# Talking-heads attention and two MLPs on one core: one bank for two head pairs' values, four banks for the first head mixing, and new numbers in the planner

## The chip, the cores and the metric

The kernel runs on one core of a Trainium2 chip. The metric is the device time of one execution in microseconds (us); lower is better. The engines are named as the profile names them: PE (TensorE matmul), PEld (its weight loads), DVE (VectorE), ACT (ScalarE), POOL (GpSimd), SP (SyncE, which issues the DMAs here). PSUM, the memory that PE writes, has eight banks of 512 float32 per partition, and every bank of this kernel belongs to a named ring.

## The reference

```python
B, H, S, D = 4, 12, 448, 64                     # q, k, v: [B, H, S, D]; w_pre, w_post: [H, H]
scores = np.matmul(q, k.transpose(0, 1, 3, 2)) / np.sqrt(D)
scores = np.einsum('bhij,hg->bgij', scores, w_pre)        # first mixing of the heads
scores = scores - np.max(scores, axis=-1, keepdims=True)
attn = np.exp(scores)
attn = attn / (np.sum(attn, axis=-1, keepdims=True) + 1e-09)
attn = np.einsum('bhij,hg->bgij', attn, w_post)           # second mixing of the heads
x = np.matmul(attn, v)                                    # the values
x = x.transpose(0, 2, 1, 3).reshape(B * S, H * D)         # [1792, 768]
h = x @ w_in;  x = (h * np.cos(h)) @ w_out                # first MLP, 2048 wide
return np.maximum(np.maximum(x @ w1, x @ w2), x @ w3) @ w_out2
```

## The kernel before

A batch's 448 rows are cut into four **scores**, blocks of 10 to 12 times 10 rows. For a score, `qk` multiplies queries and keys, two heads at a time (six per score, into two banks of the ring `ps_x`), `evac` copies each head from its bank to SBUF (on ACT or DVE), and `send` writes it by DMA into the grid `t`, where row and head lie side by side on the partitions.

A score is then worked off in **visits**, two slots of 10 rows at a time (92 in all, four of them with one slot). In a visit `mix1` (L575) mixes the heads into two banks of `ps_m`, `rowmax` (DVE) and `soft` (ACT, the exponential with its sum) make two tiles `e`, `guard`, `recip` and `wscale` (DVE) divide the second mixing's weights by the sums (tile `w2s`), `mix2` (L616) mixes again into one bank of `ps_t` for each slot, both of which it needs from its start, and `keep` (ACT or DVE) copies each bank into the buffer `a2`.

When a **stretch** of visits is complete (two scores, 220 or 230 rows), `av` (L640) multiplies its `a2` with the values, one pair of heads after the other in steps of two pairs; `keepx` (ACT or DVE, two copies a pair, tile `xs`) puts rows back in order, and `out` writes them to `xT` in memory.

Every instruction's place is set by a planner (`Plan.run`) when the kernel is built: it plays the operations through with the occupancy of each engine given in `add` (in us, `"T"` for PE, `"A"` ACT, `"V"` DVE, `"D"` DMA), a delay until the result is seen (`lands`, or one delay per engine), the rings of banks and buffers (`takes`, `frees`), a rank, and orders that must hold (`after`, `behind`). Each engine then executes its instructions in the written order and waits at whatever is not ready. An instruction waits for what the compiler found it to depend on, which need not be what the planner thought.

At the end of attention, when the last `send` has been issued, the buffers of scores are given up to the first MLP (`open_early`): its weights are fetched and cut in two parts on ACT, DVE and POOL, `xget` reads back the tokens of the first batch (in a place of `t` that the last score but one leaves free), and its matmuls (L156 to L158) fill PE between the last visits. From some point on PE runs matmuls of the MLPs without a gap.

Of the kernel before, what the change touches and what calls it, by code (L numbers as in the profile page):

```python
# [21 lines left out]
RI = 10  # L22
# [3 lines left out]
HALVES = [[[10, 12], [12, 11]]] * B  # L26
NHALF = 230
RT = 12
RH = RI // 2
BUFS = {"k": 10, "q": 9, "s": 8, "e": 5, "w2s": 3, "v": 7, "xs": 6, "a2": 2, "ps_m": 3, "ps_t": 3, "ps_x": 2}  # L30
# [413 lines left out]
def attention(ctx, tc, q, k, v, w_pre, w_post, same_row, xT, tp, mlps):  # L444
# [36 lines left out]
    for b, sizes in enumerate(HALVES):  # L481
        i = 0
        for n, half in enumerate(sizes):
            start, column = i, 0
            for slots in half:
                i = min(i, S - RI * slots)
                score.append((b, i, RI * slots, slots, 2 * b + n, column))
# [143 lines left out]
    def av(half, x, _):  # L631
        b, _, _, m, _ = halves[half]
        a2 = live["a2", half]
        for hp in pairs(x):
            vt = live["v", b, hp]
            live["av", hp] = ps_t.tile([128, JB, H, RI], F32, name="aps")
            ps = live["av", hp] = live["av", hp].rearrange("p j g i -> p (j g i)")
            for j in range(JB):
                for g in range(2):
                    nc.tensor.matmul(ps[64 * g:64 * g + 64, :m], vt[:, j, g, :], a2[:, j, 2 * hp + g, :m],  # L640
# [18 lines left out]
    def add(f, a, rank, engines, after=(), turn=False, **kw):  # L659

        key = f.__name__, *a
        plan.add(key, rank, partial(f, *a), engines, after, behind=before.get(f, ()) if turn else (), **kw)
# [3 lines left out]
    HP = H // 2  # L666

# [7 lines left out]
    for n in range(NS):  # L675
        b = score[n][0]
        start, end = score[n - 1][0] != b or not n, n == NS - 1 or score[n + 1][0] != b
        for hp in range(HP):
# [6 lines left out]
            add(qk, (n, hp), r, {"T": 0.8}, [("qget", b, hp), ("kget", b, hp)], turn=True, takes=[ring] * 2,  # L685
                frees=[(f, (f + "get", b, hp)) for f in "kq"] if end else [])
            for h in range(2 * hp, 2 * hp + 2):
                add(evac, (n, h), r, {"A": 0.55, "V": 0.62}, [("qk", n, hp)], turn=True, takes=[place := copy_place(n, h)[0]], frees=[(ring, ("qk", n, hp), h % 2)])
                if h == 0:
                    plan.add(("new_t", n), r, lambda _: None, {}, [("evac", n, 0)], takes=["t"])  # L690
                add(send, (n, h), r, {"D": score[n][2] / 118.0}, [("evac", n, h), ("new_t", n)], turn=True, frees=[(place, ("evac", n, h))], lands=2.5)


    for y, (n, t, slots) in enumerate(visits):
        i = 2 * y
        key = lambda f, *x: (f, y, *x)
        add(mix1, (y,), i, {"T": 0.8}, [("wmix", 0), ("fill", n % 2)] + [("send", n, h) for h in range(H)], turn=True, takes=["ps_m"] * 2,
            frees=[("t", ("new_t", n))])
# [3 lines left out]
        add(guard, (y,), i, {"V": 0.12}, [key("soft", a) for a in range(2)])  # L702
        add(recip, (y,), i, {"V": 0.12}, [key("guard")])
        add(wscale, (y,), i, {"V": 0.25}, [key("recip"), ("wmix", 1)], turn=True, takes=["w2s"])
        add(mix2, (y,), i + 1.5, {"T": 0.05 + 0.45 * len(slots)}, [key("wscale")], turn=True, takes=["ps_t"] * len(slots),
            frees=[("e", key("soft", a)) for a in range(2)] + [("w2s", key("wscale"))])
# [6 lines left out]
    for half, (b, _, _, _, members) in enumerate(halves):  # L713
        last = (first + [N])[members[-1] + 1] - 1
        ends = [("keep", y, a) for y, x in enumerate(visits) if x[0] in members for a in x[2]]
        start = ends[0]
        for x in range(HP // 2):
            r = last + 2.5 + 3.0 * x
            for hp in pairs(x) if half % 2 == 0 else ():
# [495 lines left out]
```

## Time and profile before

| | us |
|---|---|
| median of 3 runs | 1171.14 (1169.19 to 1177.53) |
| the profiled execution | 1172.04 |
| its span, first to last instruction | 1170.3 |
| PE busy in the span | 1130.7 |
| DVE busy | 992.9 |
| ACT busy | 656.3 |
| attention, until PE runs only MLP matmuls | 387.9 |

A busy PE is not a PE at its best: matmuls are pipelined and their ends are modelled, so a short stall is hidden in a row that looks busy. The time from the start of one group of matmuls to the start of the next says more. The granted clock of PE was 0.996 of full speed over the span.

### The profile page before, as it was taken

The numbers are of one execution on the slowest core, as the hardware profiler recorded it, in microseconds if no ns is written. First come the engines' busy times: TensorE is split into PE (matmuls) and PEld (weight loads), VectorE is DVE, ScalarE is ACT, GpSimd is POOL, SyncE is SP. The second block draws the span as 40 slices with busy tenths as digits, with TensorE's granted clock in tenths as the row PEclk, the third lists the DMA queues.
The fourth block names the chain that finished last, engine by engine and source line by source line (L and its number), as shares of the span: only waits on it lengthen the run. The fifth ranks groups of instructions, "written<-read, shape, count | busy, mean of one in ns | idle before, by whom it ended". The sixth has DMA issues, their size and how long they took to land.

```text
span 1170.3 us, 29431 instructions
## 1 busy us (share of the span) xinstructions
PE 1130.7 (97%) x11836; PEld 926.5 (79%) x11836; DVE 992.9 (85%) x2083; ACT 656.3 (56%) x1468; POOL 79.8 (7%) x69
## 2 busy tenths in 40 slices
PE   7899999899898899999999999999999999999998
PEld 2566566565556699999999999999999999999987
DVE  5878777777778899999999999997788679778994
ACT  3656556655657687555555555555534354445472
POOL 4000000000005110000000000000001021011110
PEclk9999999999999999999999999999999999999999
DMA  6785565645553655343434344431002221222233
GB/s 220 226 242 163 169 195 158 185 132 153 155 170 116 213 155 149 115 136 115 135 115 135 115 135 121 130 108 34 1 28 82 61 67 35 76 66 69 82 117 113
DMA packets 90696, 146.02 MB, mean 125 GB/s; under 512 B 8928, under 2 KB 73536, under 8 KB 90560
## 3 DMA queue, kind: packets, MB, share of 16 engines
q1 hardware_dynamic: 90304, 144.12, 40.8%
q8 instruction: 93, 1.52, 0.5%
q14 instruction: 43, 0.35, 0.1%
q0 software_dynamic: 256, 0.02, 0.0%
HBM read 84.96 MB, written 20.45 MB: 90 GB/s over the span
## 4 chain that ended last, share of the span: by engine, by line
PE 84%; DMA 6%; DVE 5%; issue 1%; ACT 1%; SPq 1%; ACTq 0%; DVEq 0%
PE ps L156 21%; PE ps L158 21%; PE ps L157 21%; PE mps L575 6%; PE aps L640 5%; PE aps L616 5%; PE ps L552 4%; DMA t<-s 3%; DMA x<-xT 1%; DVE nm L583 1%; DMA v<-in_v_dram 1%; DVE s L460 1%; DMA wraw<-in_w_in_dram 0%; ACT e L589 0%; DVE a L460 0%
## 5 line engine op out<-in xcount | busy, mean ns | idle before, releaser
L158 PE MATMUL ps<-x,w 128*128 128x448 f32 x816 | 300.0, 368 | 2.4 <-DVE x L147 1.5
L156 PE MATMUL ps<-x,w 128*128 128x448 f32 x816 | 300.4, 368 | 0.8 <-ACT gh L857 0.6
L157 PE MATMUL ps<-x,w 128*128 128x448 f32 x816 | 299.8, 367 | 0.5 <-DVE w L296 0.3
L156 PEld LDWEIGHTS ps<-x,w 128*128 128x128 f32 x816 | 153.7, 188 | 17.6 <-issue 2.4
L158 PEld LDWEIGHTS ps<-x,w 128*128 128x128 f32 x816 | 153.6, 188 | 17.4 <-POOL x L147 2.0
L157 PEld LDWEIGHTS ps<-x,w 128*128 128x128 f32 x816 | 153.7, 188 | 14.8 <-POOL w L131 0.8
L589 ACT ACTIVATE e<-mps,nm 128x448 f32<-128x448 f32 (+1 forms) x184 | 116.9, 637 | 79.2 <-DVE nm L583 59.3
L616 PEld LDWEIGHTS aps<-w2s,e 60*64 60x64 f32 x5760 | 108.7, 136 | 51.2 <-issue 23.8
L156 PE MATMUL ps<-gh,w 128*128 128x448 f32 x384 | 140.9, 367 | 0.0
L157 PE MATMUL ps<-gh,w 128*128 128x448 f32 x384 | 140.7, 366 | 0.0
L158 PE MATMUL ps<-gl,w 128*128 128x448 f32 x384 | 140.4, 366 | 0.0
L583 DVE TENSOR_REDUCE nm<-mps 128x1 f32<-128x448 f32 (+1 forms) x184 | 110.2, 616 | 30.8 <-PE mps L575 29.3
L293 ACT CAST w<-wf 128x384 fp32r<-128x384 f32 x168 | 81.1, 514 | 74.5 <-DVE wf L285 54.2
L616 PE MATMUL aps<-w2s,e 60*64 60x60 f32 x5760 | 112.7, 220 | 8.9 <-DVE w2s L603 6.2
L575 PE MATMUL mps<-t,w 64*64 64x448 f32 (+1 forms) x720 | 106.4, 558 | 10.2 <-DMA t<-s 6.2
L552 PE MATMUL ps<-k,q 64*64 64x448 f32 (+3 forms) x736 | 99.0, 551 | 5.1 <-ACT s L460 2.5
L814 DVE TENSOR_TENSOR acc<-ps,acc 128x448 f32<-128x448 f32 x168 | 100.2, 615 | 1.4 <-PE ps L158 1.4
L252 ACT ACTIVATE wf<-wraw 128x384 f32<-128x384 f32 x112 | 61.9, 553 | 51.3 <-DMA wraw<-in_w_out_dram 37.7
L296 DVE TENSOR_TENSOR w<-wf,w 128x384 fp32r<-128x384 f32 x132 | 73.7, 579 | 19.1 <-ACT w L293 18.3
L296 POOL TENSOR_TENSOR w<-wf,w 128x384 fp32r<-128x384 f32 x36 | 42.1, 1177 | 684.6 <-DVE wt L256 371.8
L640 PE MATMUL aps<-a,v 128*64 128x220 f32 (+1 forms) x768 | 78.0, 356 | 4.7 <-ACT xs L460 3.2
L640 PEld LDWEIGHTS aps<-a,v 128*64 128x64 f32 x768 | 54.2, 136 | 34.2 <-issue 5.9
(121 smaller groups left out, 1736.7 us busy)
## 6 DMA issues: line engine op xcount, KB each, us to landing
t<-s SPq DMA_DIRECT2D x96, 210.0 KB
wf<-w SPq DMA_DIRECT2D x96, 192.0 KB
wraw<-in_w_out_dram SPq DMA_DIRECT2D x44, 384.0 KB
wraw<-in_w_dram SPq DMA_DIRECT2D x36, 384.0 KB
wraw<-in_w_in_dram SPq DMA_DIRECT2D x32, 384.0 KB
t<-s SPq DMA_DIRECT2D x48, 192.5 KB
w<-wf SPq DMA_DIRECT2D x48, 192.0 KB
t<-s SPq DMA_DIRECT2D x43, 175.0 KB
```

Source lines behind the costliest of these rows:

```text
L156: mm(w[0], x[0], start=first, stop=False)
L157: mm(w[1], x[0], start=False, stop=False)
L158: mm(w[0], x[1], start=False, stop=last)
L293: return nc.scalar.copy(A[x][0], w())
L296: return eng.tensor_sub(A[x][1], w(), f32(A[x][0]))
L552: nc.tensor.matmul(live["s", n, 2 * hp + g][r:end], live["q", b, hp][half, i0 + r:i0 + end], live["k", b, hp][half], start=True, stop=True)
L575: nc.tensor.matmul(live["m", v, a][64 * y:64 * y + 64], w1[k], grids[n % 2][k, t + y, :], start=True, stop=True)
L583: nc.vector.tensor_reduce(nm, of(v, live["m", v, a]), axis=AX.X, op=ALU.max, negate=True)
L589: nc.scalar.activation(of(v, e), of(v, live["m", v, a]), AF.Exp, bias=live["nm", v, a], scale=1.0, accum_out=live["z", v][:, a:a + 1])
L616: nc.tensor.matmul(live["a", v, y][64 * c:64 * c + 64, j, :, a, :], live["e", v, a][k, o:o + 64], live["w2s", v][k, a], start=True, stop=True)
L640: nc.tensor.matmul(ps[64 * g:64 * g + 64, :m], vt[:, j, g, :], a2[:, j, 2 * hp + g, :m], start=j == 0, stop=j == JB - 1)
L814: return nc.vector.tensor_add(acc, po, acc) if fg else nc.scalar.copy(acc, po)
```

## The change

The sizes of the stretches of the first and the last batch become three (100, 120 and 230 rows, and in the last batch the other way round). `ps_m` grows from three banks to four and `ps_t` shrinks from three to two; the `s` ring loses a tile to the `e` ring. `av` puts both pairs of heads into one bank, side by side, and so takes one bank of `ps_t` and not two; the bank is free when both pairs have been copied out. A step of values is also held behind a `mix1` of a later visit (`from_visit`), which spreads the three steps over the next stretch. Occupancies of the planner become smaller for ACT and DVE, and most operations get a delay of their own.

```diff
-HALVES = [[[10, 12], [12, 11]]] * B
+HALVES = [[[10], [12], [12, 11]], [[10, 12], [12, 11]], [[10, 12], [12, 11]], [[12, 11], [12], [10]]]
-BUFS = {"k": 10, "q": 9, "s": 8, "e": 5, "w2s": 3, "v": 7, "xs": 6, "a2": 2, "ps_m": 3, "ps_t": 3, "ps_x": 2}
+BUFS = {"k": 10, "q": 9, "s": 7, "e": 6, "w2s": 3, "v": 7, "xs": 6, "a2": 2, "ps_m": 4, "ps_t": 2, "ps_x": 2}
...
-        for hp in pairs(x):
-            vt = live["v", b, hp]
-            live["av", hp] = ps_t.tile([128, JB, H, RI], F32, name="aps")
-            ps = live["av", hp] = live["av", hp].rearrange("p j g i -> p (j g i)")
+        both = ps_t.tile([128, JB * H * RI], F32, name="aps")
+        for n, hp in enumerate(pairs(x)):
+            ps = live["av", hp] = both[:, n * NHALF:(n + 1) * NHALF]
...
-                add(evac, (n, h), r, {"A": 0.55, "V": 0.62}, [("qk", n, hp)], turn=True, takes=[place := copy_place(n, h)[0]], frees=[(ring, ("qk", n, hp), h % 2)])
+                add(evac, (n, h), r, {"A": 0.42, "V": 0.53}, [("qk", n, hp)], turn=True, lands=0.16, takes=[place := copy_place(n, h)[0]], frees=[(ring, ("qk", n, hp), h % 2)])
...
-            add(rowmax, (y, a), i, {"V": 0.6}, [key("mix1")], turn=True)
-            add(soft, (y, a), i, {"A": 0.68}, [key("rowmax", a)], turn=True, takes=["e"], frees=[("ps_m", key("mix1"), a)])
+            add(rowmax, (y, a), i, {"V": 0.53}, [key("mix1")], turn=True, lands=0.12)
+            add(soft, (y, a), i, {"A": 0.62}, [key("rowmax", a)], turn=True, takes=["e"], frees=[("ps_m", key("mix1"), a)], lands=0.14)
...
-            add(keep, (y, c), i + 1.5, {"A": 0.57, "V": 0.65}, [key("mix2")], turn=True, takes=["a2"] * begin,
+            add(keep, (y, c), i + 1.5, {"A": 0.45, "V": 0.57}, [key("mix2")], turn=True, lands=0.17, takes=["a2"] * begin,
...
-            add(av, (half, x), r, {"T": 3.25}, [("vget", b, hp) for hp in pairs(x)] + ends, turn=True, takes=["ps_t"] * 2,
-                frees=[("a2", start)] + [("v", ("vget", b, hp)) for hp in pairs(x) if half % 2])
+            add(av, (half, x), r, {"T": 0.2 + 0.0139 * halves[half][3]}, [("vget", b, hp) for hp in pairs(x)] + ends, turn=True, takes=["ps_t"],
+                frees=[("a2", start)] + [("v", ("vget", b, hp)) for hp in pairs(x) if halves[half][1] + halves[half][2] == S],
+                behind=from_visit(ylast + 2 + x * room // 3))
...
-                add(keepx, (half, hp), r, {"A": 0.45, "V": 0.5}, [("av", half, x)], turn=True, takes=["xs"], frees=[("ps_t", ("av", half, x), hp % 2)])
+                add(keepx, (half, hp), r, {"A": 0.13 * len(members), "V": 0.18 * len(members)}, [("av", half, x)], turn=True, lands=0.2,
+                    takes=["xs"], frees=[("ps_t", ("av", half, x))])
```

The delay of `send` goes from 2.5 to 3.5 and its occupancy from rows/118 to rows/125. What the planner makes of it is seen in the order of instructions. In the names, `mps` is a bank of `ps_m`, `aps` one of `ps_t`, `ps` one of `ps_x`; `a` is the buffer `a2`.

**PE, middle of the attention, around the first two steps of values of a 230-row stretch in the second batch.** Before:

```order
L575 MATMUL mps<-t,w_124 64x448 x4
L552 MATMUL ps<-k,q 64x448 x2
L552 MATMUL ps<-k,q 56x448 x2
L616 MATMUL aps<-w2s,e 64x12x5 x32
L575 MATMUL mps<-t,w_124 64x448 x4
L640 MATMUL aps<-a_2947,v_129 64x230 x8
L640 MATMUL aps<-a_2947,v_130 64x230 x8
L552 MATMUL ps<-k,q 64x448 x2
L552 MATMUL ps<-k,q 56x448 x2
L616 MATMUL aps<-w2s,e 64x12x5 x32
```

Now:

```order
L576 MATMUL mps<-t,w_124 64x448 x4
L617 MATMUL aps<-w2s,e 64x12x5 x32
L553 MATMUL ps<-k,q 64x448 x2
L553 MATMUL ps<-k,q 56x448 x2
L640 MATMUL aps<-a_3009,v_127 64x230 x8
L640 MATMUL aps<-a_3009,v_128 64x230 x8
L576 MATMUL mps<-t,w_124 64x448 x4
L617 MATMUL aps<-w2s,e 64x12x5 x32
```

In both a step of values is followed by one group (a `qk` or a `mix1`) and then by a `mix2`; what moved is which visit that `mix2` belongs to. Counted over all 92 visits, when a `mix2` begins before, three first mixings not yet mixed again have been issued 51 times and two 37 times; now four 71 times and three 16 times.

**DVE, around its share of the copies of that kind of step, with what each instruction waits for; the other pair of heads is copied by ACT.** Before, where ACT copies bank `aps_2018` and DVE bank `aps_2027`:

```order
L594 TENSOR_SCALAR z_2016<-z_2016 128x2 [waits Activation_49]
L598 RECIPROCAL rz_2048<-z_2016 128x2 [waits DVE_49]
L603 TENSOR_TENSOR w2s_2050<-w2t_125,rz_2048 128x120 [waits DVE_49]
L460 COPY xs_2062<-aps_2027 128x120 [waits PE_49]
L460 COPY xs_2062<-aps_2027 128x110 [waits DVE_49]
L583 TENSOR_REDUCE nm_2102<-mps_2053 128x1 [waits PE_49]
```

Now, where ACT copies the other half of the same bank `aps_2206`:

```order
L595 TENSOR_SCALAR z_2189<-z_2189 128x2 [waits Activation_49]
L599 RECIPROCAL rz_2230<-z_2189 128x2 [waits DVE_49]
L604 TENSOR_TENSOR w2s_2233<-w2t_125,rz_2230 128x120 [waits DVE_49]
L461 COPY xs_2256<-aps_2206 128x120 [waits PE_49,Activation_49]
L461 COPY xs_2256<-aps_2206 128x110 [waits DVE_49]
```

DVE's first copy waits for PE alone before, and for PE and ACT now: the semaphore value is that of ACT's last copy out of the bank. It is so in 24 of the 30 steps.

**PE, the end of attention: the last second mixing and what follows.** Before:

```order
L616 MATMUL aps<-w2s,e 64x12x5 x16
L640 MATMUL aps<-a_6437,v_130 64x230 x8
L640 MATMUL aps<-a_6437,v_131 64x230 x8
L640 MATMUL aps<-a_6437,v_132 64x230 x8
L640 MATMUL aps<-a_6437,v_126 64x230 x8
L640 MATMUL aps<-a_6437,v_127 64x230 x8
L640 MATMUL aps<-a_6437,v_128 64x230 x8
```

Now, after the last second mixing and six MLP matmuls:

```order
L640 MATMUL aps<-a_6977,v_130 64x100 x8
L640 MATMUL aps<-a_6977,v_131 64x100 x8
L157 MATMUL ps<-x,w 128x448
L158 MATMUL ps<-x,w 128x448
L159 MATMUL ps<-x,w 128x448
L640 MATMUL aps<-a_6977,v_132 64x100 x8
L640 MATMUL aps<-a_6977,v_126 64x100 x8
L640 MATMUL aps<-a_6977,v_127 64x100 x8
L640 MATMUL aps<-a_6977,v_128 64x100 x8
```

The last values are 100 columns wide where they were 230, and MLP matmuls stand between them.

## Rows read from the trace of the kernel before

**Rows 1.** Windows by stage: length, PE, PEld, DVE, ACT, POOL busy, PE clock, DMA share, GB/s.

```profile
23.30:98.30 75.00, 70.57 (x1796) 43.30 (x1796) 61.09 (x164) 49.08 (x136) 0.00 (x0) 1.00 0.73 219
98.30:345.30 247.00, 234.30 (x5595) 144.97 (x5593) 190.10 (x499) 147.00 (x404) 0.00 (x0) 0.99 0.55 162
345.30:387.90 42.60, 34.55 (x598) 23.59 (x588) 38.23 (x78) 31.30 (x74) 18.51 (x15) 0.96 0.44 137
```

**Rows 2.** Timeline of PE in a dense stretch: start, length, line, operation, count.

```profile
151.31 1.10 PE L616 MATMUL aps<-w2s,e 60*64 60x60 f32 x64
152.24 0.93 PE L575 MATMUL mps<-t,w 64*64 64x448 f32 x8
153.00 0.92 PE L552 MATMUL ps<-k,q 64*46 64x448 f32 x8
153.75 1.10 PE L616 MATMUL aps<-w2s,e 60*64 60x60 f32 x64
154.68 1.02 PE L575 MATMUL mps<-t,w 64*64 64x448 f32 x8
155.63 3.19 PE L640 MATMUL aps<-a,v 128*64 128x220 f32 x32
158.76 0.59 PE L552 MATMUL ps<-k,q 64*64 64x448 f32 x4
```

**Rows 3.** Groups of PE by line, 98.3 to 345.3 us: count, busy, mean, idle before.

```profile
L616 PE MATMUL aps<-w2s,e 60*64 60x60 f32 x4003 | 76.9, 220 | 3.2 <-DVE w2s L603 3.2
L575 PE MATMUL mps<-t,w 64*64 64x448 f32 (+1 forms) x504 | 71.0, 554 | 7.0 <-DMA t<-s 5.6 <-issue 0.7 <-DMA xT<-xs 0.4
L552 PE MATMUL ps<-k,q 64*64 64x448 f32 (+3 forms) x512 | 66.9, 549 | 1.7 <-DVE s L460 0.7 <-ACT s L460 0.5 <-issue 0.5
L640 PE MATMUL aps<-a,v 128*64 128x220 f32 (+1 forms) x576 | 58.7, 356 | 0.7 <-ACT a L460 0.7
```

**Rows 4.** Waits of PEld, 98.3 to 345.3 us: total, times, longest.

```profile
PEld aps L616 <- DVE w2s L603: 11.7, 15, 1.8
...
PEld mps L575 <- ACT e L589: 7.1, 13, 0.8
```

**Rows 5.** Timeline of PE, ACT and DVE: a second mixing and the copies around it.

```profile
159.56 1.10 PE L616 MATMUL aps<-w2s,e 60*64 60x60 f32 x64
160.49 0.99 PE L552 MATMUL ps<-k,q 64*64 64x448 f32 x8
...
159.84 0.62 DVE L460 COPY s<-ps 110x448 f32<-110x448 f32 x1 [0.32 <-PE ps L552]
160.76 0.66 DVE L460 COPY a<-aps 128x480 f32<-128x480 f32 x1 [0.30 <-PE aps L616]
```

**Rows 6.** Timeline of PE, ACT and DVE: a step of values and its copies.

```profile
190.82 3.33 PE L640 MATMUL aps<-a,v 128*64 128x230 f32 x32
...
192.64 0.54 ACT L460 COPY xs<-aps 128x120 f32<-128x120 f32 x2 [0.40 <-PE aps L640]
194.07 0.98 PE L575 MATMUL mps<-t,w 64*64 64x448 f32 x8
194.19 0.59 DVE L460 COPY xs<-aps 128x120 f32<-128x120 f32 x2 [1.21 <-PE aps L640]
194.88 0.34 PE L616 MATMUL aps<-w2s,e 60*64 60x60 f32 x10
```

**Rows 7.** Timeline of PE and SP: a score's last qk, last sends, next first mixing.

```profile
203.19 0.93 PE L552 MATMUL ps<-k,q 64*64 64x448 f32 x8
205.14 2.00 SPq L566 DMA_DIRECT2D t<-s  x2
211.38 0.98 PE L575 MATMUL mps<-t,w 64*64 64x448 f32 x8 [0.44 <-DMA xT<-xs]
```

**Rows 8.** Timeline of PE at the end of attention.

```profile
375.05 4.88 PE L640 MATMUL aps<-a,v 128*64 128x230 f32 x48 [0.84 <-DVE a L460]
383.09 4.88 PE L640 MATMUL aps<-a,v 128*64 128x230 f32 x48 [3.16 <-ACT xs L460]
```

More of the change, by code (lines that the diff above doesn't have):

```diff
@@ L483, in attention @@
         for n, half in enumerate(sizes):
-            start, column = i, 0
+            start, column, nhalf = min(i, S - RI * half[0]), 0, len(halves)
             for slots in half:
                 i = min(i, S - RI * slots)
-                score.append((b, i, RI * slots, slots, 2 * b + n, column))
+                score.append((b, i, RI * slots, slots, nhalf, column))
                 column += RI * slots
@@ L633, in av @@
         a2 = live["a2", half]
[L634 to L637 removed]
+        both = ps_t.tile([128, JB * H * RI], F32, name="aps")
+        for n, hp in enumerate(pairs(x)):
+            ps = live["av", hp] = both[:, n * NHALF:(n + 1) * NHALF]
             for j in range(JB):
                 for g in range(2):
[L640 removed]
+                    nc.tensor.matmul(ps[64 * g:64 * g + 64, :m], live["v", b, hp][:, j, g, :], a2[:, j, 2 * hp + g, :m],
                                      start=j == 0, stop=j == JB - 1)
@@ L657, in attention, with add @@
     before = {}
-    def add(f, a, rank, engines, after=(), turn=False, **kw):
+    def add(f, a, rank, engines, after=(), turn=False, behind=(), **kw):
         key = f.__name__, *a
-        plan.add(key, rank, partial(f, *a), engines, after, behind=before.get(f, ()) if turn else (), **kw)
+        plan.add(key, rank, partial(f, *a), engines, after, behind=list(before.get(f, ()) if turn else ()) + list(behind), **kw)
         if turn:
@@ L666, in attention, with from_visit @@
     HP = H // 2
+    starts = [next(y for y, x in enumerate(visits) if x[0] == n) for n in range(NS)] + [len(visits)]
+    def from_visit(y):
+        return [("mix1", y)] if 0 <= y < len(visits) else []
     for x in range(3):
@@ L696, in attention @@
         key = lambda f, *x: (f, y, *x)
-        add(mix1, (y,), i, {"T": 0.8}, [("wmix", 0), ("fill", n % 2)] + [("send", n, h) for h in range(H)], turn=True, takes=["ps_m"] * 2,
+        add(mix1, (y,), i, {"T": 0.78}, [("wmix", 0), ("fill", n % 2)] + [("send", n, h) for h in range(H)], turn=True, takes=["ps_m"] * 2,
             frees=[("t", ("new_t", n))])
         for a in range(2):
-            add(rowmax, (y, a), i, {"V": 0.6}, [key("mix1")], turn=True)
-            add(soft, (y, a), i, {"A": 0.68}, [key("rowmax", a)], turn=True, takes=["e"], frees=[("ps_m", key("mix1"), a)])
[L702 to L705, printed above, removed]
+            add(rowmax, (y, a), i, {"V": 0.53}, [key("mix1")], turn=True, lands=0.12)
+            add(soft, (y, a), i, {"A": 0.62}, [key("rowmax", a)], turn=True, takes=["e"], frees=[("ps_m", key("mix1"), a)], lands=0.14)
+        add(guard, (y,), i, {"V": 0.07}, [key("soft", a) for a in range(2)], lands=0.13)
+        add(recip, (y,), i, {"V": 0.07}, [key("guard")], lands=0.13)
+        add(wscale, (y,), i, {"V": 0.19}, [key("recip"), ("wmix", 1)], turn=True, takes=["w2s"], lands=0.135)
+        add(mix2, (y,), i + 1.5, {"T": 0.04 + 0.465 * len(slots)}, [key("wscale")], turn=True, takes=["ps_t"] * len(slots),
             frees=[("e", key("soft", a)) for a in range(2)] + [("w2s", key("wscale"))])
@@ L714, in attention @@
         last = (first + [N])[members[-1] + 1] - 1
+        ylast = starts[members[-1] + 1] - 1
+        room = min(12, starts[halves[half + 1][4][-1] + 1] - 1 - ylast) if half + 1 < len(halves) else 12
         ends = [("keep", y, a) for y, x in enumerate(visits) if x[0] in members for a in x[2]]
@@ L935, in attention @@
         r = (r0, N - 1)[n] + RANK[("fx", "x1")[n]]
-        add(xget, (n,), r, {"D": 3.6}, [("out", 2 * n + x, hp) for x in range(2) for hp in range(H // 2)] + [("xget", 0)] * n
+        add(xget, (n,), r, {"D": 3.6}, [("out", x, hp) for x, y in enumerate(halves) if y[0] == n for hp in range(H // 2)] + [("xget", 0)] * n
             + [("block", FG)], takes=["t"])
```

6 lines of the change are left out of this document (3 added, 3 removed).

## The prediction

> **What bounds the kernel now.** I read the stages first. The last 758 us are a dense run of MLP matmuls, which the change does not touch, so what it can give lies before 387.9 us, and there DVE is busy for 77% of the middle stage (190.1 of 247.0 us), ACT for 60% [rows 1]: no engine but PE is near its limit, yet PE does not run at its own. Its busy time hides that, so I compare starts with starts. In a dense stretch a `mix2` takes 0.93 us (151.31 to 152.24), a `mix1` 0.76, a `qk` 0.75, a step of values 3.13 (155.63 to 158.76) [rows 2], and 3.25 where it is 230 wide (190.82 to 194.07) [rows 6]. The groups by line count two instructions for a float32 matmul, so 64 of L616, 8 of L575 and L552 and 32 of L640 make one group [rows 3]. From 98.3 to 345.3 us that is 62.5 `mix2`, 63 `mix1`, 64 `qk` and 18 steps of values: 58.1 + 47.9 + 48.0 + 57.4 = 211.4 us of work in 247.0 us. **35.6 us are lost**, only 12.7 of them as visible idle time (247.0 - 234.3) [rows 1].
>
> What PE waits for there is told best by its weight loads, which wait ahead of the matmuls: 11.7 us for `w2s`, the end of the chain `mix1`, `rowmax`, `soft`, `guard`, `recip`, `wscale`, and 7.1 us for a `soft` that still holds a bank of `ps_m` [rows 4]; PE itself idles 5.6 us for grids `t` on their way [rows 3]. So the loss is one of distance and banks: the order gives a visit too little other work between its two mixings.
>
> **What the change takes away.** By the order, with the floors above, the PE work between the end of a visit's `mix1` and the start of its `mix2` has a median of 5.3 us before and 10.6 us now; its lowest tenth goes from 4.0 to 5.5. The first mixing runs a visit further ahead, which the fourth bank allows: a bank's next `mix1` came at most 1.7 us of work after the last use's end in 54 of 91 visits before, and does so in two now. I take both waits of [rows 4] as gone. Not the whole 35.6 us goes, since the change leaves some waits and brings others. For the 63 visits of this stage (17 steps of values now, 16 of them with other work behind) I count these.
>
> *Steps of values.* The `mix1` ahead of one takes 0.95 us (154.68 to 155.63) [rows 2] and the `qk` behind it 0.80 (158.76 to 159.56) [rows 2, 5], 0.24 above the floors together. 17 steps: 4.1 us.
>
> *One bank for both pairs.* Before, ACT copies the first pair out (192.64) while PE still multiplies the second, and DVE copies the second pair 0.12 us after the step's end, for 0.59 us [rows 6]. Now ACT's copies wait for the whole step, and DVE's wait for ACT's, as the order's waits show, which the planner's numbers do not know. The bank is free 0.12 + 0.54 + 0.12 + 0.59 + about 0.1 for the signal = 1.5 us after the step. A `mix2` that needs both banks stands one group behind the step (0.81 us: 194.07 to 194.88 [rows 6]), so it waits 0.7 us; in 220-row stretches, whose copies are shorter, about 0.5. With 0.6 for 16 steps: **9.6 us** of new waiting; between 0, if PE would have waited there anyway, and 11.
>
> The Trainium skill's page "PSUM — Partial Sum Buffer", section "PSUM bank collisions raise a hardware error", says that any two of TensorE, ScalarE and VectorE which touch one bank on the same partitions at once collide, so that a program must order them, even two readers; it speaks against this edit. The trace of before can't show it, since there each pair had its own bank. Could the two copy at once after the step, the term would be about 0.1 a step and the sum below 8 us better.
>
> *Two banks of `ps_t`, not three.* A bank is copied out 0.93 us after its `mix2`'s end (160.49 to 160.76 + 0.66) [rows 5], about 1.0 with the signal. Where two groups (1.5 us) stand between two `mix2` nothing waits; where one stands (9 places) it waits some 0.27: 2.4 us.
>
> *A `qk` soon after a `qk`.* Its banks are copied out 0.9 us after the first one's end (159.56 to 159.84 + 0.62) [rows 5]; with a `mix2` of 0.93 between them (11 places, 7 before) it waits about 0.1: 1 us.
>
> *The grids.* From the last `qk` of a score (ends 203.95) over the send's issue (until 207.14) to the first `mix1` (211.38) are 7.4 us [rows 7]. The order puts 5.4 to 9.0 us of PE work there now, at the 11 such places; what falls short of 7.4 sums up to 13 us, and to 22 by the same count before, when PE idled 5.6 us for it [rows 3], since other waits stretch the work. In proportion 3.3; I take 4, with 13 as the bound.
>
> The sum is 4.1 + 9.6 + 2.4 + 1 + 4 = 21.1 us left of 35.6: **14.5 us gained**. DVE's own waiting for ACT, up to 0.66 us a step, costs nothing while its idle 57 us of this stage cover it; without that cover it would be up to 10. The bounds: 10 us left if these waits fall together (a gain of 25), 32 if the highest value holds everywhere (a gain of 4).
>
> **The other stages.** Until 98.3 us the queue of DMAs is the tighter one, 0.73 of its engines at 219 GB/s against 0.55 at 162 later [rows 1]. The order on SP now puts four pairs of value tiles among the sends of the second score, which all stood behind them before: 0.9 MB, 4.1 us at that rate, of which other work covers some. I take +1, from -2 to +4. The two batches with a third stretch have 6 more steps of values with the same columns in all: 6 x 0.24 = +1.4. At the end PE waits 0.84 and 3.16 us for copies between its last values, 230 wide [rows 8]; now the last are 100 wide, with MLP matmuls between them. But DVE is busy for 38.2 of the 42.6 us from 345.3 to 387.9 [rows 1], and its work there stays, so the stage can hardly shrink by more than 4.4 us: I take -4, from 0 to -8 where conversions move past the end. The smaller occupancies cost nothing by themselves; they act through the order, which is counted above.
>
> Together -14.5 + 1 + 1.4 - 4 = -16 us: 1172.0 of the profiled execution becomes 1156, and as the median of the runs is 0.9 us lower, **1155**.
>
> **The rivals.** *Nothing is left to win.* The new waits take the place of the old: the highest values above give -4 + 4 + 1.4, about 1172. For it speaks that the planner does not know of the ordered copies, and that [rows 8] show how a copy that stands behind others holds up values for 3 us; against it, that stretches without any loss exist, [rows 2] among them, with less distance than the new order has everywhere.
>
> *The waits share their time.* A PE that waits for a bank gives the grids time to land. With 10 us left, 8 at the end and nothing in the first stage the gain is 25 + 8 - 1.4, so about 1140. The even spread of the values over a stretch speaks for it.
>
> *Two value banks are too few, and it gets slower.* A `mix2` takes both, so every one waits for both copies of the one before. If a copy stands behind two others of 0.66 us on its engine, its bank is free 2.3 us after the `mix2`, and after the usual two groups the next one waits 0.85 us. At 40 of the 92 visits that is 34 us, 1189. It cancels the gain from 19 visits on and is slower by over 1% from 33 on. For it: occupancies without reserve leave such a copy no slack. Against it: in [rows 5] both kinds of copy begin 0.3 us after their matmuls, and DVE and ACT have room. The Trainium skill's page "Perfetto Trace Analysis", section "Optimizing Tensor Performance", asks that independent groups of matmuls rotate through different banks so that one is copied out while the next runs; with two banks that a group takes together there is no such rotation, and no run here shows yet what that costs.
>
> **Chances.** A measurement of this kernel tells about 1% from no change: 1159.4 and 1182.9 are the lines. The forecast (1147 to 1164) 0.53; nothing to win (1165 to 1176) 0.21; shared waits (1138 to 1147) 0.17; slower 0.09. About 0.38 of the forecast's 0.53 lies below 1159.4. Faster 0.55, same 0.37, slower 0.08. The range from 1140 to 1171 leaves out the slower case and the tails.
>
> **What would show it.** Right: weight loads of L617 no longer wait for `w2s`; between two batches' first mixings the middle stage shrinks by some 14 us; behind a step of values the `mix2` starts 1.5 us after it, released by DVE's copy of `xs`, which itself begins after ACT's. Wrong: waits of L617 for copies of `a` at ordinary visits (the slower rival), a first batch that lasts 4 us longer, or an end of attention in which PE waits for tokens `x`. A middle stage without waits behind values would make it faster than I say.

## The result and the profile after

The changed kernel takes 1156.33 us in the median (1149.53 to 1159.13, four runs), the kernel before 1170.16 us beside it: a ratio of 0.9867, 95% interval 0.9827 to 0.9907. The profiled execution went from 1172.04 to 1158.33 us, its span from 1170.3 to 1156.5. Two executions on record, the profiled one of `after_again` below (1232.65 us) and one of before, ran at a granted clock of 0.849 throughout and stand in no ratio, median or stage below.

The stages of the kernel after, cut where the first mixings of visits 0, 23 and 87 start, and at 387.9 us (columns as in [rows 1]; lines of the two kernels differ by one, so L616 of before is L617 here):

```profile
23.00:98.80 75.80, 69.72 (x1836) 46.72 (x1829) 59.23 (x157) 52.43 (x142) 0.00 (x0) 0.98 0.74 214
98.80:336.10 237.30, 228.06 (x5558) 156.62 (x5559) 178.33 (x482) 153.88 (x423) 0.00 (x0) 0.99 0.56 167
336.10:387.90 51.80, 47.71 (x841) 38.46 (x840) 45.81 (x95) 38.27 (x90) 14.13 (x11) 0.93 0.54 172
```

Against [rows 1] the first stage is 0.8 us longer (75.8 against 75.0), the middle 9.7 shorter (237.3 against 247.0), and what follows visit 87 takes 820.4 us of the span (1156.5 - 336.1) against 825.0. So 9.7 + 4.6 - 0.8 = 13.5 of the 13.8 us by which the span shrank; the first 23 us hold the rest.

The groups of PE by line in that middle stage (columns as in [rows 3]):

```profile
L617 PE MATMUL aps<-w2s,e 60*64 60x60 f32 x3968 | 83.2, 220 | 7.7 <-issue 4.3 <-DVE xs L461 2.7
L553 PE MATMUL ps<-k,q 64*64 64x448 f32 (+3 forms) x512 | 67.2, 543 | 0.3
L576 PE MATMUL mps<-t,w 64*64 64x448 f32 (+1 forms) x502 | 66.4, 551 | 1.9 <-ACT a L461 0.9 <-DMA q<-in_q_dram 0.5 <-issue 0.3
...
```

The waits for `w2s` and for grids `t` of [rows 3] are gone. New are `xs`, the copies of values, and 4.3 us of "issue", in which PE waited for nothing that the profile shows. Of the two waits of [rows 4] the weight loads have 0.2 us left for `w2s` (once) and 0.5 for the `soft`; their longer waits are these:

```profile
PEld aps L617 <- issue: 21.6, 73, 2.5
...
PEld aps L640 <- ACT a L461: 7.4, 10, 1.1
...
PEld aps L617 <- ACT a L461: 2.6, 5, 0.7
PEld aps L617 <- DVE a L461: 2.1, 5, 0.6
```

A step of values, to be laid beside [rows 6] (timeline, all engines, lines of other work left out):

```profile
300.65 1.72 PE L640 MATMUL aps<-a,v 128*64 128x230 f32 x16
...
302.43 0.54 ACT L461 COPY xs<-aps 128x120 f32<-128x120 f32 x2 [2.23 <-PE aps L640]
...
303.00 0.59 DVE L461 COPY xs<-aps 128x120 f32<-128x120 f32 x2 [1.96 <-ACT xs L461]
...
303.11 0.28 PE L617 MATMUL aps<-w2s,e 60*64 60x60 f32 x4
...
303.73 1.09 PE L617 MATMUL aps<-w2s,e 60*64 60x60 f32 x58 [0.34 <-DVE xs L461]
```

ACT copies only after the whole step, DVE only after ACT, and the `mix2` stops after its first few matmuls until DVE has done: DVE ends at 303.59, 1.28 us after the step (302.31, where `qk` starts). It is the picture that the prediction drew, but for the `mix2`, which starts 0.8 us behind the step, in the free bank, and waits inside. At the end, PE multiplies values 120 and 100 wide with MLP matmuls between, where it waited 0.84 and 3.16 us in [rows 8]:

```profile
364.55 1.86 PE L640 MATMUL aps<-a,v 128*64 128x120 f32 x32
366.35 0.47 PE L157 MATMUL ps<-x,w 128*128 128x448 f32 x1
...
370.59 1.59 PE L640 MATMUL aps<-a,v 128*64 128x100 f32 x32 [0.23 <-DVE a L461]
...
372.92 2.97 PE L640 MATMUL aps<-a,v 128*64 128x100 f32 x64
```

### The profile page after: what moved, and what is told of

Same layout as the page of the kernel before. It is cut to its first block, busy times and chain, and to the rows that moved or that the text cites. A ratio compares the mean times of both kernels' runs of the same rounds, so it can differ in the third digit from the quotient of the medians.

```text
span 1156.5 us, 29873 instructions
## 1 busy us (share of the span) xinstructions
PE 1124.7 (97%) x12028; PEld 944.2 (82%) x12028; DVE 979.4 (85%) x2057; ACT 667.0 (58%) x1497; POOL 76.0 (7%) x66
## 4 chain that ended last, share of the span: by engine, by line
PE 88%; DVE 6%; DMA 3%; issue 2%; ACT 1%; SPq 0%; DVEq 0%; ACTq 0%
PE ps L157 21%; PE ps L159 21%; PE ps L158 21%; PE aps L617 7%; PE mps L576 6%; PE aps L640 6%; PE ps L553 5%; DVE nm L584 1%; DMA k<-in_k_dram 1%; DMA wraw<-in_w_in_dram 1%; DMA t<-s 1%; DVE xs L461 0%; DVE x L148 0%; DVE s L461 0%; DVE x L334 0%
## 5 line engine op out<-in xcount | busy, mean ns | idle before, releaser
L158 PEld LDWEIGHTS ps<-x,w 128*128 128x128 f32 x816 | 153.3, 188 | 13.8 <-DVE w L297 0.7
L617 PEld LDWEIGHTS aps<-w2s,e 60*64 60x64 f32 x5760 | 118.6, 136 | 48.0 <-issue 28.9
L617 PE MATMUL aps<-w2s,e 60*64 60x60 f32 x5760 | 119.9, 221 | 12.3 <-issue 8.0
L590 ACT ACTIVATE e<-mps,nm 128x448 f32<-128x448 f32 (+1 forms) x184 | 116.4, 645 | 14.0 <-DVE nm L584 11.8
L294 ACT CAST w<-wf 128x384 fp32r<-128x384 f32 x168 | 81.1, 514 | 73.7 <-DVE wf L286 55.1
L584 DVE TENSOR_REDUCE nm<-mps 128x1 f32<-128x448 f32 (+1 forms) x184 | 107.5, 616 | 17.1 <-PE mps L576 15.7
L553 PE MATMUL ps<-k,q 64*64 64x448 f32 (+3 forms) x736 | 101.7, 557 | 4.4 <-ACT s L461 2.0
L576 PE MATMUL mps<-t,w 64*64 64x448 f32 (+1 forms) x720 | 96.5, 562 | 4.6 <-DMA k<-in_k_dram 1.7
L253 ACT ACTIVATE wf<-wraw 128x384 f32<-128x384 f32 x112 | 61.9, 553 | 56.4 <-DMA wraw<-in_w_out_dram 35.5
L640 PEld LDWEIGHTS aps<-a,v 128*64 128x64 f32 x960 | 58.8, 138 | 30.6 <-ACT a L461 11.5
L461 ACT COPY a<-aps 128x480 f32<-128x480 f32 x104 | 58.1, 574 | 44.0 <-PE aps L617 43.9
```

The source lines that it names most:

```text
L158: mm(w[1], x[0], start=False, stop=False)
L294: return nc.scalar.copy(A[x][0], w())
L553: nc.tensor.matmul(live["s", n, 2 * hp + g][r:end], live["q", b, hp][half, i0 + r:i0 + end], live["k", b, hp][half], start=True, stop=True)
L576: nc.tensor.matmul(live["m", v, a][64 * y:64 * y + 64], w1[k], grids[n % 2][k, t + y, :], start=True, stop=True)
L584: nc.vector.tensor_reduce(nm, of(v, live["m", v, a]), axis=AX.X, op=ALU.max, negate=True)
L590: nc.scalar.activation(of(v, e), of(v, live["m", v, a]), AF.Exp, bias=live["nm", v, a], scale=1.0, accum_out=live["z", v][:, a:a + 1])
```

## The experiments

The change has four parts: banks (four, two, both pairs in one), numbers (occupancies and delays), three stretches of values in the outer batches, and the spread, the rule that holds a step of values behind a later visit's `mix1`. A fifth, the tile that the `s` ring gives to the `e` ring, was not varied: the kernels built from before lack it (`banks_alone`, `numbers_alone`, `occupancies`, `numbers_three`), those built from after have it. `banks_alone` and `numbers_alone` do one part alone, `two_stretches` and `no_spread` undo one. The table holds all twelve runs beside before and after; the ratios are to the kernel before on the same chip. The stage lengths come from one profiled execution of each, cut at the first mixings of visits 23 and 87; the loss is the middle's length minus its groups of matmuls at the prediction's floors, since kernels move a step of values across a cut. "Distance" is the median measured time from the last matmul of a visit's `mix1` to the first of its `mix2` in the middle.

| kernel | median us | ratio (95%) | to 23 | 23 to 87 | loss in it | after 87 | distance |
|---|---|---|---|---|---|---|---|
| before | 1170.2 | 1 | 75.0 | 247.0 | 35.5 | 825.0 | 6.6 |
| after | 1156.3 | 0.9867 (0.9827 to 0.9907) | 75.8 | 237.3 | 26.3 | 820.4 | 12.1 |
| banks_alone | 1192.6 | 1.0193 (1.0162 to 1.0224) | 82.1 | 260.0 | 47.8 | 824.1 | 7.4 |
| numbers_alone | 1158.3 | 0.9885 (0.9856 to 0.9914) | 79.0 | 232.1 | 23.7 | 824.2 | 6.0 |
| occupancies | 1158.0 | 0.9900 (0.9873 to 0.9928) | 76.8 | 233.8 | 24.2 | 822.5 | 6.7 |
| numbers_three | 1152.2 | 0.9850 (0.9826 to 0.9875) | 81.1 | 228.9 | 20.1 | 818.7 | 6.0 |
| without_banks | 1161.9 | 0.9923 (0.9896 to 0.9951) | 79.8 | 233.5 | 22.5 | 824.0 | 7.8 |
| two_stretches | 1175.1 | 1.0055 (1.0032 to 1.0078) | 80.6 | 244.9 | 37.5 | 827.9 | 11.0 |
| no_spread | 1170.6 | 0.9978 (0.9949 to 1.0006) | 85.9 | 239.4 | 33.8 | 818.8 | 6.9 |
| three_three | 1170.4 | 1.0015 (0.9990 to 1.0040) | 80.3 | 246.2 | 35.2 | 817.4 | 6.7 |
| own_banks | 1156.5 | 0.9893 (0.9858 to 0.9927) | 75.4 | 225.9 | 19.1 | 828.9 | 12.4 |
| own_then_shared | 1150.0 | 0.9842 (0.9814 to 0.9869) | 75.3 | 230.1 | 23.3 | 825.7 | |
| one_copy | 1158.6 | 0.9895 (0.9857 to 0.9933) | 76.7 | 241.4 | 32.2 | 814.7 | |
| after_again | 1157.9 | 0.9898 (0.9873 to 0.9922) | | | | | |

In `own_banks`, `own_then_shared` and `two_stretches` some 4 us of work (a step of values and a `mix2`), and in `no_spread` some 5, are done after visit 87 instead of before, which their last stage holds.

**banks_alone.** The kernel before with the new banks.

```diff
-"ps_m": 3, "ps_t": 3, "ps_x": 2}
+"ps_m": 4, "ps_t": 2, "ps_x": 2}
...
+        both = ps_t.tile([128, JB * H * RI], F32, name="aps")
+        for n, hp in enumerate(pairs(x)):
+            ps = live["av", hp] = both[:, n * NHALF:(n + 1) * NHALF]
...
-            add(av, (half, x), r, {"T": 3.25}, ..., turn=True, takes=["ps_t"] * 2,
+            add(av, (half, x), r, {"T": 3.25}, ..., turn=True, takes=["ps_t"],
```

> The kernel before with four banks for the first mixing, two for the second, and both pairs' values in one bank; its numbers, stretches and order rules stay. First theory (the fourth bank gives the distance between a visit's two mixings, and with it the gain): most of the 14 us come, about 1160 us. Rival (the distance comes from where the values steps are put): by the order the median work between the mixings is 5.6 us here, as before (5.3), and 34 second mixings stand one group or less behind another against 18, so no gain, 1168 to 1176 us; 34 x 0.27 + 18 x 0.5 = 18 us of new waits against some 19 us of old ones.

1.9% slower than before: both theories missed, and the first fell. Its weight loads in the middle (106.6 to 366.6 us; waits of PEld: total, times, longest), and who waited at the copies `xs`:

```profile
PEld aps L616 <- ACT a L460: 11.6, 21, 0.8
PEld mps L575 <- ACT e L589: 8.6, 11, 1.7
...
PEld mps L575 <- DMA t<-s: 6.2, 3, 3.1
...
PEld aps L616 <- DVE a L460: 2.4, 3, 0.8
```

```profile
its engine sat idle before it (us, times) until:
  ACT xs L460: 37.1, 18
  PE aps L639: 31.5, 18
```

L639 is the line of the values here. The waits for `w2s` are gone from the first list too, those for a `soft` are not (8.6 us against 7.1 in [rows 4]), and 12.3 us more are lost than before. The 14.0 us of waits for copies of `a` are what the prediction's slower rival named as its sign. Of the loss, 23 `mix2` that stand one group behind another lost 14.7 us, 21 with two groups between 8.5.

Some of it is the clock. Three times in this middle PE lost 2.5 to 3 us at one place and soon after worked for 3.4 us at about half its clock, the level of 1.2 GHz; so here (columns as in [rows 1]):

```profile
176.20:180.20 4.00, 1.65 (x16) 0.61 (x18) 1.88 (x6) 1.58 (x4) 0.00 (x0) 1.00 0.84 239
180.20:183.60 3.40, 3.40 (x80) 2.39 (x76) 2.01 (x4) 1.91 (x5) 0.00 (x0) 0.54 0.42 150
```

The groups in the three such stretches lost some 5 us of the 47.8, those in the one of before (at 142.5 us) some 1.6 of 35.5. Over the whole kernel the six runs of `banks_alone` have a granted clock of 0.982 to 0.986, those of before beside them 0.993 in the mean. If PE had work all the time, this alone would be 0.0095 x 1190, an estimate of 11 of the 22 us; no run separates it.

**numbers_alone.** The kernel before with every occupancy and delay of the kernel after, nothing else.

```diff
-                add(evac, (n, h), r, {"A": 0.55, "V": 0.62}, ...
+                add(evac, (n, h), r, {"A": 0.42, "V": 0.53}, ..., lands=0.16, ...
...
-            add(rowmax, (y, a), i, {"V": 0.6}, [key("mix1")], turn=True)
+            add(rowmax, (y, a), i, {"V": 0.53}, [key("mix1")], turn=True, lands=0.12)
...
-            add(keep, (y, c), i + 1.5, {"A": 0.57, "V": 0.65}, ...
+            add(keep, (y, c), i + 1.5, {"A": 0.45, "V": 0.57}, ..., lands=0.17, ...
```

> The kernel before with the planner's occupancies and delays of the kernel after; banks, stretches and the place of values steps stay. First theory (banks): no change, 1166 to 1173 us. Rival (an order planned with measured numbers loses less by itself): about 1160 us. By the order the median work between the mixings is 4.9 us here against 5.3 before, which speaks for no change.

The rival was right: the numbers alone bring the gain (0.9885, against 0.9867 and 0.9898 of the kernel after), with three banks and a shorter distance than before. The waits of its weight loads in the middle (103.8 to 335.9 us):

```profile
PEld aps L616 <- DVE w2s L603: 16.6, 23, 1.3
```

16.6 us of waiting for `w2s`, more than the 11.7 of [rows 4], in a stage that loses 11.8 us less. Such waits are not the loss: PE itself idled 2.8 us for `w2s` here and 3.2 in [rows 3].

**two_stretches** and **no_spread.** The kernel after without one of its parts.

```diff
-HALVES = [[[10], [12], [12, 11]], [[10, 12], [12, 11]], [[10, 12], [12, 11]], [[12, 11], [12], [10]]]
+HALVES = [[[10, 12], [12, 11]]] * B
```

```diff
-                frees=[...],
-                behind=from_visit(ylast + 2 + x * room // 3))
+                frees=[...])
```

> The kernel after with two stretches of values in every batch, as before the change. If the three stretches serve the end alone, the end loses the 4.2 us that it gained and 6 values steps go, so 1158 to 1160 us. Rival (the shorter stretches are what lets the values spread): distance falls from 10.6 to 8.7 us in the median, 31 tight second mixings against 16, so 4 to 8 us more in the middle too, 1162 to 1168 us.

> The kernel after without the rule that holds a values step behind the first mixing of a later visit. First theory (banks): little is lost, 1156 to 1160 us, since the fourth bank is still there. Rival (the spread makes the distance): by the order the median distance falls to 5.6 us and 25 second mixings are tight, so most of the gain goes, 1166 to 1172 us.

Without the stretches the kernel is slower than before, beyond both guesses: the first stage is 4.8 us longer, 3.5 us go at the end (827.9 less the 4 us of moved work, against 820.4), but 11 in the middle, though the distance stays at 11.0 us. Without the spread most of the gain goes, as the rival said, but not by distance alone: the first stage is 10.1 us longer than that of after (its granted clock 0.93 against 0.98), the middle loses 7.5 more, and the end is shorter. Of its twelve runs eight took 1168 to 1174 us and four 1162 to 1164. Since `numbers_alone` has neither stretches nor spread and keeps its gain, it is with the new banks that the order needs both.

**without_banks**, **three_three** and **own_banks.** With the kernel after itself these are the four cases of two questions: three and three banks, or four and two; each pair's values in a bank of its own, or both in one. `three_three` has the first of these edits, `own_banks` the second, `without_banks` both:

```diff
-"ps_m": 4, "ps_t": 2, "ps_x": 2}
+"ps_m": 3, "ps_t": 3, "ps_x": 2}
```

```diff
-        both = ps_t.tile([128, JB * H * RI], F32, name="aps")
-        for n, hp in enumerate(pairs(x)):
-            ps = live["av", hp] = both[:, n * NHALF:(n + 1) * NHALF]
+        for hp in pairs(x):
+            live["av", hp] = ps_t.tile([128, JB, H, RI], F32, name="aps")
...
-            add(av, ..., takes=["ps_t"], frees=...
+            add(av, ..., takes=["ps_t"] * 2, frees=...
```

> The kernel after with the banks of before: three for each mixing, and each pair's values in a bank of its own; numbers, stretches and spread as after. The measured numbers alone gave 1158 us with the old banks, the banks alone 1193. First theory (numbers and three stretches bring the gain, the banks nothing): 1150 to 1156 us, numbers_alone less the end's 4 us. Rival (the spread needs the fourth bank, without which visits can't run ahead): distance 7.2 us instead of 10.6 and 31 tight second mixings instead of 16, so 1160 to 1167 us.

> The kernel after with three banks for each mixing instead of four and two; both pairs' values stay in one bank. If the fourth bank matters: the median distance falls from 10.6 to 4.9 us, waits for banks that soft holds come back (7 us of weight loads in before), 1163 to 1170 us. If the third bank of the second mixing matters as much (3.3 us of waits of second mixings that stand one group apart, and the ordered copies hidden by a free bank): 1152 to 1158 us.

> The kernel after (four and two banks), but each pair's values have one of the two banks of their own. Theory of the prediction (ordered copies out of one bank cost the second mixing behind a step 0.57 us, 0.29 in 220-wide stretches): about 7 us in the middle and 2 elsewhere go, 1147 to 1151 us. Rival (the step must now wait at its start for both banks, which a second mixing's copies hold 1.0 us): 24 steps by 0.3 to 0.5 come in its place, 1153 to 1160 us.

Three banks with own banks give 1161.9, three with a shared one 1170.4, four and two with own banks 1156.5, with a shared one 1156.3 and 1157.9. `without_banks` and `own_banks` lie in the ranges of their rivals, `three_three` just above the one for a fourth bank that matters: with the spread and the third stretch in place, the old banks keep only 0.8% of gain. So a shared bank costs 0.9% where there are three of the first mixing, and nothing in the sum where there are four. But in the middle `own_banks` loses 7.2 us less than after. Who waits there at the copies `xs`, first in the kernel after (98.8 to 336.1 us), then in `own_banks` (98.7 to 324.6):

```profile
its engine sat idle before it (us, times) until:
  PE aps L640: 35.2, 17
  ACT xs L461: 30.6, 17
who waited for it (us, times):
  DVE xs L461: 30.6, 17
  PE aps L617: 2.7, 8
```

```profile
its engine sat idle before it (us, times) until:
  PE aps L641: 39.3, 31
  DMA t<-s: 1.1, 1
```

In after, DVE's copies waited for ACT's at all 17 steps, and PE's `mix2` for DVE's; with own banks neither is left. The `mix2` behind a step lost 7.2 us at 16 steps in after, 1.3 at 16 in `own_banks`. More than half of what the middle saved was given back at the end (828.9 less the 4 us of moved work, against 820.4), where small steps that each take both banks now wait for copies (timeline of PE in `own_banks`):

```profile
358.62 1.86 PE L641 MATMUL aps<-a,v 128*64 128x120 f32 x32 [1.12 <-ACT a L461]
...
361.60 1.30 PE L617 MATMUL aps<-w2s,e 60*64 60x60 f32 x64 [1.12 <-ACT xs L461]
...
364.77 5.96 PE L641 MATMUL aps<-a,v 128*64 128x100 f32 x95 [1.87 <-DVE a L461]
```

**one_copy.** Both pairs of a step leave their bank in one instruction for each score, on one engine; the `xs` ring has three tiles of twice the size in place of six.

```diff
-            for hp in pairs(x):
-                add(keepx, (half, hp), r, {"A": 0.13 * len(members), "V": 0.18 * len(members)}, ...
+            add(keepx, (half, x), r, {"A": 0.365 * len(members), "V": 0.45 * len(members)}, ...
```

> The kernel after, but one engine copies both pairs of a step out of their bank in one instruction for each score (two for a 230-wide stretch) instead of ACT and behind it DVE. From the copies' times (480 columns 0.574, 120 columns 0.259 us on ACT) one of 240 columns takes some 0.37 us, so the bank is free 0.95 us after the step instead of 1.5. Theory of the prediction (ordered copies cost 0.57 us a step): 1148 to 1152 us. Rival (what a changed order brings outweighs it; 29 tight second mixings instead of 16): 1156 to 1162 us.

Inconclusive for the bank's price. The copies are as short as expected (0.348 us in the median on ACT, which makes them all), but the order changed with them: the middle lost 32.2 us, among them two breaks of 3.0 and 1.8 us (see the last section), some 3.4 in a stretch of 6.8 us at half clock behind the first of them, and 2.4 in which a `mix1` waited for a transfer out of `xs`. The time is that of the rival.

**own_then_shared.** As `own_banks`, but the last two stretches share a bank.

```diff
+        shared = half >= len(halves) - 2
...
-            add(av, ..., takes=["ps_t"] * 2, frees=...
+            add(av, ..., takes=["ps_t"] * (2 - (half >= len(halves) - 2)), frees=...
```

> The kernel own_banks (each pair's values in a bank of its own), but the steps of the last two stretches share a bank as in the kernel after. own_banks reached the first mixing of visit 87 at 324.6 us, after at 336.1, of which one step of 3.3 us that own_banks had still to do; its total was only 3 us shorter. Theory (the sharing costs 7 us in the middle, and own banks lose 4 us at the end, where two banks serve small steps that each take both): the middle keeps its 7 us and the end its 4, so 1151 to 1153 us, some 4 under after_again. Rival (the end is bound by DVE's copies and conversions, whatever the banks): no change from own_banks, 1155 to 1157 us.

The total is 1 us under the theory's range: 1150.0 us, below `after_again` on the same chip with intervals that do not quite meet (with that of after's first measurement it does meet). In the profiles the last stage is 3.2 us shorter than that of `own_banks`. The half on the middle is not shown: the profiled execution, 1156.99 us, was the longest of its six, and its middle of 230.1 us holds breaks that `own_banks` has not.

**numbers_three.** As `numbers_alone`, with the three stretches.

```diff
-HALVES = [[[10, 12], [12, 11]]] * B
+HALVES = [[[10], [12], [12, 11]], [[10, 12], [12, 11]], [[10, 12], [12, 11]], [[12, 11], [12], [10]]]
```

> The kernel before with the measured numbers and the three stretches of values in the first and last batch; banks and the place of values steps as before. numbers_alone (1158 us) lost nothing to after in the middle (232.1 against 237.3 us between the first mixings of visits 23 and 87) but its end was 4 us longer. Theory (the stretches serve the end): 1153 to 1156 us. Rival (without the spread, or with three banks, the small stretches stall on their copies as in without_banks): 1159 to 1163 us.

1152.2 us, 0.8 under the theory's range, and the last stage is 5.5 us shorter than in `numbers_alone` (818.7 against 824.2); the intervals of the two ratios still overlap. This kernel is after without the new banks, the spread and the tile for `e`, and is as fast as the best: on top of numbers and stretches those bring nothing in the time.

**occupancies.** As `numbers_alone`, without the delays.

```diff
-                add(evac, ..., lands=0.16, ...
+                add(evac, ...
...
-                add(send, ..., lands=3.5)
+                add(send, ..., lands=2.5)
```

> The kernel before with the measured occupancies alone; the delays after each operation stay the planner's general ones and those of the sends 2.5 us. If the gain of numbers_alone comes from occupancies without reserve (an order that fits how long DVE and ACT are really busy): 1156 to 1161 us. If it comes from the delays (which set when a result is seen by the next engine, and the 3.5 us of a send): no gain, 1166 to 1172 us.

1158.0 us: the occupancies alone do it. The new ones are what the trace of before shows from the start of an instruction to the start of the next where the engine has no gap (timelines of DVE and ACT):

```profile
155.53 0.62 DVE L460 COPY s<-ps 110x448 f32<-110x448 f32 x1
156.07 0.16 DVE L598 RECIPROCAL rz<-z 128x2 f32<-128x2 f32 x1
...
163.63 0.56 ACT L460 COPY a<-aps 128x480 f32<-128x480 f32 x1
164.07 0.64 ACT L589 ACTIVATE e<-mps,nm 128x448 f32<-128x448 f32 x1
```

The copy on DVE lasts 0.62 us, but the next instruction starts after 0.54; that on ACT lasts 0.56, and the next starts after 0.44. The old numbers, 0.62 and 0.57, are such lengths; the new ones, 0.53 and 0.45, such distances.

What they moved is seen in the copies of `s` and `a` (groups by line in the middle; first before, then `occupancies`):

```profile
L460 DVE COPY s<-ps 120x448 f32<-120x448 f32 (+2 forms) x83 | 50.0, 618 | 4.3 <-PE ps L552 3.6
L460 ACT COPY s<-ps 120x448 f32<-120x448 f32 (+2 forms) x47 | 24.7, 533 | 16.6 <-PE ps L552 16.4
```

```profile
L460 DVE COPY s<-ps 120x448 f32<-120x448 f32 (+2 forms) x69 | 42.5, 619 | 5.1 <-PE ps L552 4.9
L460 ACT COPY s<-ps 120x448 f32<-120x448 f32 (+2 forms) x59 | 31.6, 536 | 9.7 <-PE ps L552 9.7
```

With 0.42 against 0.53 us instead of 0.55 against 0.62 the planner gives ACT 12 more of these copies and DVE 14 fewer. `numbers_alone` has 60 and 68, after 58 and 70. That the relief of DVE is the cause was not tried by itself; the planner's times also move everything else. The loss itself shrank most behind `qk`: from the start of a `qk` to that of the next group 14.0 us are lost in the middle of before, 6.9 in `occupancies`; behind `mix1` 8.5 and 7.2, behind `mix2` 12.2 and 7.3, behind values 0.8 and 2.7. The banks alone move it: 15.7, 4.3 and 28.2 in `banks_alone`.

**after_again.** The kernel after, unchanged.

> The kernel after once more, beside the three others. 1153 to 1159 us, as before. If the two breaks of 2.1 and 2.6 us in the middle of a second mixing, behind which nothing is seen to be waited for, belong to the order of its code, they stand at the same visits (34 and 54) again; if they are chance, elsewhere or nowhere.

1157.9 us in the median, as expected. At visits 34 and 54 it has no break. At visit 87 both executions stop for over 2 us behind the same instruction, the 24th of the 64 of its `mix2` (timeline of PE, first after, then `after_again`):

```profile
343.24 0.57 PE L617 MATMUL aps<-w2s,e 60*64 60x60 f32 x24
346.07 0.93 PE L617 MATMUL aps<-w2s,e 60*64 60x60 f32 x40 [2.26 <-issue]
```

```profile
362.91 0.59 PE L617 MATMUL aps<-w2s,e 60*64 60x60 f32 x24
365.95 0.84 PE L617 MATMUL aps<-w2s,e 60*64 60x60 f32 x40 [2.44 <-issue]
```

So neither of the two expectations fits by itself: the place belongs to the code, but not every such place breaks in every execution.

## Why the prediction was right in its sum and wrong in its cause

The forecast of 1155 us was 1.3 us low, and the profiled execution fell by 13.7 us where 16 were summed. That it came so near is in part luck: below, terms are off by up to 5 us, and the errors cancel. By its terms:

*Stages.* First stage +0.8 (said +1, and half of the 1.4 for six more steps). End -4.6 (said -4), by the way said: narrow last values with MLP matmuls between. The stretches do this, as `numbers_three` shows by itself.

*Middle.* The loss went from 35.5 to 26.3 us, not to 21.1. What stands ahead of the 17 steps lost 3.6, what stands behind them 0.8 (said 4.1 together). The `mix2` behind 16 steps lost 7.2 (said 9.6): 0.57 in 230-wide stretches and 0.3 in 220-wide ones where 0.7 and 0.5 were taken. The order of copies in one bank, on which the sum was weighed with the Trainium skill's page "PSUM — Partial Sum Buffer", section "PSUM bank collisions raise a hardware error", is there as the page has it: DVE stood 30.6 us behind ACT, at every step; what two copies without an order would do no run here shows. The ten `mix2` one group behind another lost 3.5 without a break (said 2.4 at nine), the 38 with two groups between 5.1 (said nothing). The other `qk` lost 0.7 (said 1). Grids cost nothing that PE shows (said 4). Two breaks (last section) took 4.3 in the profiled execution (not foreseen). The rest is about 1. In all, some 1.6 us of these fell into the 3.4 us at half clock behind the second break.

*The cause.* The step that failed is "The first mixing runs a visit further ahead, which the fourth bank allows", and with it taking both waits of [rows 4] for the loss. Those waits did go but for 0.7 us, and the distance nearly doubled (12.1 us measured against 6.6), but neither is what was gained: `banks_alone` takes the `w2s` waits away and is 22 us slower, `two_stretches` has a distance of 11.0 us and no gain, and `numbers_alone` keeps these waits (16.6 and 2.9 us, against 11.7 and 7.1 before), at a distance of 6.0, and has the gain; `occupancies`, as fast, has half of them (6.3 and 3.3). A weight load that waits runs ahead of the matmuls and often costs them nothing: 16.6 us of them stand beside 2.8 us of PE's own idle time. "The smaller occupancies cost nothing by themselves; they act through the order" was right, but it led me to count the order of all parts together and to credit the banks.

*The rivals.* "Two value banks are too few", at 1189 us, is what the banks do with the old numbers: 1192.6, with the waits for copies of `a` that it named. The Trainium skill's page "Perfetto Trace Analysis", section "Optimizing Tensor Performance", asks for groups that rotate through different banks; `banks_alone`, which takes a bank from that rotation and makes two pairs share one, agrees with it by 1.9%, while `own_then_shared`, with the same two banks and a better order, is as fast as `numbers_three` with three (0.9842 and 0.9850). "Nothing is left to win" is `no_spread` and `three_three`.

*Left open.* Which of the occupancies brings the gain, and whether by DVE's load. Whether the kernel after needs them: after with the old numbers was not run, so the numbers are shown to be enough, not to be the only way. What the tile for `e` does, which no kernel varies alone. Why `two_stretches` loses 11 us in the middle with so much distance was not tried further.

## What to carry to other kernels

Where a planner orders the work, correct its numbers alone and time that before giving it banks or rules: here the measured occupancies were worth 12 us and, with them, the stretches 4 to 6 (not clear of the noise in the total), while banks that cost 22 us by themselves were made good by the rest. The occupancy to give it is the distance from start to start, not an instruction's length. Compare granted clocks beside times: the long waits of `banks_alone` came back as stretches at half clock. Judge a loss by the starts of matmuls against their dense floors; weight loads that wait, and the distance between two dependent steps, rose and fell here without the time. A sum of terms that comes out right does not show which part earned it; one kernel for each part does.

## What was not expected of the hardware

PE can stop in the middle of a `mix2` whose operands and banks are all there. The timeline of PE in the kernel after:

```profile
146.62 0.92 PE L617 MATMUL aps<-w2s,e 60*64 60x60 f32 x44
149.46 0.45 PE L617 MATMUL aps<-w2s,e 60*64 60x60 f32 x16 [1.92 <-issue]
...
223.14 1.14 PE L617 MATMUL aps<-w2s,e 60*64 60x60 f32 x54
226.66 0.44 PE L617 MATMUL aps<-w2s,e 60*64 60x60 f32 x10 [2.38 <-issue]
```

Four such breaks of 1.4 to 2.6 us, from the matmul ahead to the one behind, stand before 345 us in the profiled execution of after, one of 1.5 in that of before, none in that of `occupancies`. `own_banks` and `own_then_shared` have the same order up to their ends, and both break behind the same matmul in the `mix2` of visit 4 (idle for 1.6 and 0.8 us) and of visit 26 (1.7 and 1.0); `own_then_shared` has others of 1.0 to 1.4 us idle where `own_banks` has at most 0.4. So the place belongs to the code and the length to the execution.

A late piece of code would do that, and the times of the transfers on the instruction queue bear it out (the page of after counts 94 of them). In the fourteen profiles of this case 40 gaps of 0.95 us or more from one matmul to the next, inside a group and with no wait that the profile shows, stand before 390 us; every one ends 1.2 to 1.8 us after such a transfer has ended. There are 62 to 65 transfers in that time, so that an arbitrary moment stands so behind one in a tenth of the cases. No run changed the fetching of code, so what else could stop PE there is not excluded. The four take some 8 us of the profiled execution of after, more than half of the effect that was measured.

The clock can fall after such a break. Windows of the kernel after (columns as in [rows 1]), during the break at 223 us and behind it:

```profile
223.10:227.10 4.00, 1.62 (x72) 1.45 (x71) 1.19 (x4) 1.53 (x6) 0.00 (x0) 1.00 0.68 200
227.10:230.50 3.40, 3.40 (x76) 2.40 (x80) 2.04 (x5) 1.24 (x3) 0.00 (x0) 0.51 0.96 244
```

PE, busy for 1.62 of 4.0 us, then worked for 3.4 us at 0.51 of its clock, the level of 1.2 GHz. Such a stretch also stands behind the break at 344 us (346.4 to 349.8 us, clock 0.53). The break of 2.1 us at 147 us was followed by none, nor were the shorter ones of `own_then_shared`.
